# Fused pooled attention and rational MoE: zero-adding fill matmuls, shifted due times and a lead for the key transposes

## The chip, the cores and the metric

The kernel runs on one core of one Trainium2 chip. The metric is the time of one execution in device microseconds (us), the median of several runs. The profile is one further execution; its span is the time from the first instruction to the last.

## The reference, cut to what matters

Attention over keys and values pooled by 8, then a two-matrix network with a rational activation (all float32):

```python
B, H, S, D = 8, 8, 576, 64              # Sp = S // 8 = 72 pooled keys
k_p = k.reshape(B, H, Sp, 8, D).mean(axis=3);  v_p = v.reshape(B, H, Sp, 8, D).mean(axis=3)
attn = softmax(D ** -0.5 * q @ k_p.T)            # with 1e-9 added to the sum
x = (attn @ v_p).transpose(0, 2, 1, 3).reshape(4608, 512)
h = x @ w_in                                      # w_in 512 x 2048
g = (a0 + a1*h + a2*h**2 + a3*h**3) / (1 + |b0|*|h| + |b1|*h**2 + 1e-6)
out = g @ w_out                                   # w_out 2048 x 512
```

## The kernel before, in words

**Tiles.** The 4608 tokens are 18 blocks of 256. A block i goes through attention (scores `ps`, exponentials `e`, their transposes `pm` and `pr`, the split probabilities `am0` and `am1`, the products `pv`, and the split result `x0`, `x1`), then through 8 slices u of 256 hidden columns: `ph` = x times `win`u, the rational function on ScalarE, VectorE and GpSimd (tiles `t`, `w`, `r`, `rp`, giving `gh` and `gl`), and `po` += g times `wout`u. Float32 precision comes from splitting each operand in a high and a low part and adding three products. A `po` sum of a block takes two of the 8 PSUM banks (`po`i`_0`, `po`i`_1`) and stays open over its slices. The order table starts with blocks 0 and 1 on slices 0 to 3, then 2 and 3, while the weights still arrive; each weight is decoded (`m_win`, `m_wout`: ScalarE, then two VectorE instructions; then the high part by ScalarE and the low part by GpSimd).

**What sets the order.** The program isn't written in its final order. Each operation is recorded as an `Op` with a cost, its dependencies and a due time; `solve` moves due times backwards through the dependencies, then simulates the engines and always takes the operation that can start first, weighted a little by its due time. `issue` emits the operations in that order, so every engine runs a fixed list, in order, and waits on semaphores.

**The fill.** The planner also knows where TensorE has nothing to do. There `issue` puts matmuls of the identity (line 264 of the profile, tile `idle`) that nobody reads, one for each 0.12 us of the planned gap. They write the bank `idle`, which stays taken until a last operation on it that is due at 96; later, up to `FILL` = 110, they write the first bank of the next operation if that is still unused. All real work has line 267.

Of the kernel before, what the change touches and what calls it, by code (L numbers as in the profile page):

```python
# [8 lines left out]
F32 = mybir.dt.float32  # L9
F32R = mybir.dt.float32r  # L10
# [84 lines left out]
class Op:  # L95
    __slots__ = ("eng", "cost", "port", "calls", "deps", "users", "bufs", "due", "wait",
                 "ready", "seq", "bytes", "early", "slack", "start", "end")


class Plan:  # L100
# [5 lines left out]
    FILL = 110.0  # L106

    BETA = 0.02
# [13 lines left out]
    def add(self, eng, cost, calls, port=False, claims=(), bytes=0, early=34.0, after=()):  # L122
        op = Op()
        op.eng, op.cost, op.port, op.calls, op.bytes = eng, cost, port, calls, bytes
        op.early, op.slack = early, self.slack
# [28 lines left out]

    def solve(self):
        for op in reversed(self.ops):
            for d in op.deps:
                d.users.append(op)
                d.due = min(d.due, op.due - d.slack * (d.cost + 0.25 + (4.0 if d.bytes else 0.0)))
        for op in self.ops:  # L160
            op.wait, op.ready = len(op.deps), max(0.0, op.due - op.early)
# [9 lines left out]
        while done < len(self.ops):  # L171
# [35 lines left out]
            t, op = best  # L207
# [22 lines left out]
            for u in op.users:  # L230
                u.wait -= 1
                u.ready = max(u.ready, op.end + (self.LAT if u.eng != op.eng else 0.0))
                if not u.wait:
                    engs[u.eng].append(u)
# [4 lines left out]
    def issue(self):  # L239
        for op in self.order:  # L240
            for b in op.bufs:
                b.it = None
        engines = {"sp": self.nc.sync, "act": self.nc.scalar, "actq": self.nc.scalar,
                   "dve": self.nc.vector, "pool": self.nc.gpsimd, "pe": self.nc.tensor}
        value = lambda v: v.ap() if isinstance(v, Lazy) else v
        free, steady = None, [o.start for o in self.order if self.idle.tile in o.bufs][-1]
        for op in self.order:
            if op.eng == "pe" and op.start <= self.FILL:


                to = self.idle.ap() if op.start <= steady else None
                dst = op.calls[0][1][0]
                if to is None and dst.tile.it is None and dst.tile.dtype == F32:
                    to = dst.ap()
                one = self.filler
                if to is not None and tuple(to.shape) != (128, 128):
                    one = one.unsqueeze(1).to_broadcast([128, 2, 128])
                    if tuple(to.shape) not in ((128, 256), (128, 2, 128)):
                        to = None
                while free is not None and to is not None:  # L260
                    free += 0.12 if free > self.WARM else 0.215
                    if free > op.start - (0.0 if op.start <= steady else 0.2):
                        break
                    self.nc.tensor.matmul(to, lhsT=self.filler, rhs=one, start=True, stop=True)  # L264
                free = op.end
            for name, args, kw in op.calls:
                getattr(engines[op.eng], name)(*map(value, args),  # L267
                                               **{k: value(v) for k, v in kw.items()})
# [17 lines left out]
def tile_pooled_attention_then_rational_moe(  # L286
# [16 lines left out]
    nc = tc.nc  # L303
# [61 lines left out]
    ident = identr.bitcast(F32)  # L365
    masks = new("cpool", "masks", [P, 6], F32, "masks")
# [101 lines left out]
    def prep_k(n):  # L468
# [5 lines left out]
        for c0, c1, np in ((0, 2, P), (2, 4, P), (4, 5, H * SP - 4 * P)):  # L474
# [9 lines left out]
            while w > D:  # L484
# [8 lines left out]
            pe(109 * nc_, [  # L493
                ("transpose", (pk[:, (c0 + c) * P:(c0 + c + 1) * P] if c0 < 4 else pl[:, 0:np],
                               ks[:, c].rearrange("p a d -> p (a d)"), ident[:np, :np]), {})
                for c in range(nc_)])
        dst, both = kpT[n % 2], 2 * SP
# [407 lines left out]
    plan.now = 96.0  # L905
# [33 lines left out]
    plan.filler = identr  # L939
    plan.solve()  # L940
    with tc.manual_schedule():
        make_identity(nc, ones)
        nc.vector.tensor_copy(identr, ones)
        nc.gpsimd.memset(cbias, QC)
        plan.issue()
# [32 lines left out]
```

## Time and profile before

| | |
|---|---|
| median of 3 runs | 952.19 us (951.56 to 952.34) |
| the profiled execution's own time | 953.93 us |
| its span | 952.2 us |
| TensorE busy, fill matmuls included | 938.5 us |
| VectorE, ScalarE, GpSimd busy | 791.5, 691.6, 523.3 us |
| fill matmuls of 256 columns | 156 |

A fill matmul counts as busy. So the busy time of TensorE doesn't tell how much of it is work; its stretches with fill are read in the timeline, where a row is a run of like instructions with its start and length, and in brackets what the engine sat idle for before it.

### The profile page before, as it was taken

The page shows a single profiled execution, that of the slowest core. Times are in us where ns is not written, and L with a number is a line of the kernel's source. Part 1 is how long each engine was busy: PE and PEld are TensorE (multiplying, and loading weights), DVE is VectorE, ACT ScalarE, POOL GpSimd, SP SyncE. Part 2 cuts the span into 40 slices and gives each one's busy share as a digit, 9 for nine tenths or more (in the row PEclk, how much of TensorE's full clock was granted, in tenths as well). Part 3 has the DMA queues.
Part 4 walks back from the last instruction along what each step waited for, and adds up shares of the span by engine and source line. Part 5 has one row for each costly group of instructions (what it writes and reads, how often), then busy time and mean ns, then how long its engine had stood idle before and what let it go on. Part 6 is the DMA issues. An engine that isn't in the chain of part 4 may idle for free.

```text
span 952.2 us, 14488 instructions
## 1 busy us (share of the span) xinstructions
PE 938.5 (99%) x4888; PEld 786.1 (83%) x4888; DVE 791.5 (83%) x1334; ACT 691.6 (73%) x1124; POOL 523.3 (55%) x463
## 2 busy tenths in 40 slices
PE   8999999999999999999999999999999999999997
PEld 7989999898878888877887888878887888888886
DVE  6978888988898888888888989888979878886664
ACT  4778788687767686767777686858586868586764
POOL 4676667874456453547454844465456544444442
PEclk9999999999999999999999999999999999999999
DMA  9993110551436130316031512162223312020001
GB/s 280 345 384 120 24 50 1 120 149 49 89 64 148 19 60 12 66 51 141 5 68 50 122 33 43 41 135 55 32 53 74 71 26 53 0 56 1 23 1 45
DMA packets 185354, 75.16 MB, mean 79 GB/s; under 512 B 162624, under 2 KB 162624, under 8 KB 185280
## 3 DMA queue, kind: packets, MB, share of 16 engines
q1 hardware_dynamic: 185280, 74.23, 31.6%
q8 instruction: 39, 0.64, 0.3%
q14 instruction: 35, 0.29, 0.1%
HBM read 50.60 MB, written 12.58 MB: 66 GB/s over the span
## 4 chain that ended last, share of the span: by engine, by line
PE 84%; DVE 6%; ACT 3%; SPq 2%; DMA 2%; issue 2%; POOL 1%; ACTq 0%; POOLq 0%; DVEq 0%
PE po L267 37%; PE ph L267 36%; PE pv L267 4%; PE ps L267 3%; SPq L267 2%; DVE t L267 2%; PE idle L264 1%; DVE m_win L267 1%; DVE sm L267 1%; DMA q<-in_q_dram 1%; PE pvs L267 1%; DMA st_v<-in_v_dram 1%; DVE e L267 1%; ACT t L267 1%; ACT rp L267 1%
## 5 line engine op out<-in xcount | busy, mean ns | idle before, releaser
L267 PE MATMUL ph<-x,win 128*128 128x512 f32 (+1 forms) x2112 | 469.9, 354 | 4.8 <-DVE t L267 1.8
L267 PEld LDWEIGHTS ph<-x,win 128*128 128x128 f32 x2112 | 355.1, 188 | 72.6 <-DVE t L267 3.6
L267 PE MATMUL po<-wout,gh 128*128 128x512 f32 x1152 | 329.6, 397 | 0.3 <-ACT gh L267 0.3
L267 POOL TENSOR_TENSOR w<-w,r 128x512 f32<-128x512 f32 (+1 forms) x145 | 190.8, 1316 | 243.4 <-ACT r L267 228.9
L267 PEld LDWEIGHTS po<-wout,gh 128*128 128x128 f32 x1152 | 208.5, 188 | 42.1 <-ACT gh L267 0.5
L267 POOL TENSOR_TENSOR gl<-t,gh 128x512 fp32r<-128x512 f32 (+1 forms) x145 | 189.0, 1304 | 97.3 <-ACT gh L267 93.5
L267 PE MATMUL po<-wout,gl 128*128 128x512 f32 x576 | 167.6, 397 | 0.0
L267 ACT ACTIVATE t<-ph,abn 128x512 f32<-128x512 f32 (+1 forms) x145 | 111.7, 771 | 41.0 <-PE ph L267 30.8
L267 ACT ACTIVATE rp<-w,cbias 128x512 f32<-128x512 f32 (+1 forms) x145 | 99.7, 688 | 57.4 <-POOL w L267 24.3
L267 DVE TENSOR_TENSOR t<-t,ph 128x512 f32<-128x512 f32 (+1 forms) x145 | 98.4, 678 | 50.0 <-ACT t L267 48.0
L267 DVE SCALAR_TENSOR_TENSOR t<-t,abn,rp 128x512 f32<-128x512 f32 (+1 forms) x145 | 106.7, 736 | 35.2 <-ACT rp L267 33.8
L267 ACT ACTIVATE r<-w,abn 128x512 f32<-128x512 f32 (+1 forms) x145 | 117.7, 812 | 20.7 <-POOL gl L267 12.2
L267 PEld LDWEIGHTS po<-wout,gl 128*128 128x128 f32 x576 | 105.5, 189 | 21.9 <-issue 0.2
L267 DVE SCALAR_TENSOR_TENSOR t<-t,abn,ph 128x512 f32<-128x512 f32 (+1 forms) x145 | 107.5, 741 | 8.5 <-ACT w L267 4.7
L267 ACT ACTIVATE w<-ph 128x512 f32<-128x512 f32 (+1 forms) x145 | 85.9, 592 | 38.3 <-PE ph L267 29.8
L267 ACT CAST gh<-t 128x512 fp32r<-128x512 f32 (+1 forms) x145 | 88.4, 609 | 23.7 <-DVE t L267 23.4
L267 DVE SCALAR_TENSOR_TENSOR t<-rp,t 128x512 f32<-128x512 f32 (+1 forms) x145 | 99.0, 683 | 4.0
L267 DVE SCALAR_TENSOR_TENSOR rp<-w,rp 128x512 f32<-128x512 f32 (+1 forms) x145 | 99.2, 684 | 0.5 <-ACT rp L267 0.5
L267 ACT ACTIVATE rp<-rp 128x512 f32<-128x512 f32 (+1 forms) x145 | 84.1, 580 | 3.3 <-DVE t L267 0.5
L267 POOL TENSOR_TENSOR e<-e,sm 128x576 f32<-128x576 f32 x36 | 41.5, 1160 | 52.5 <-DVE sm L267 34.2
L267 PE MATMUL pv<-am,vm 128*128 128x256 f32 (+3 forms) x288 | 47.8, 278 | 0.5 <-ACT rp L267 0.4
L267 PEld LDWEIGHTS ps<-kpT,qT 128*128 128x128 f32 (+1 forms) x320 | 39.7, 178 | 9.5 <-issue 4.1
(95 smaller groups left out, 829.8 us busy)
## 6 DMA issues: line engine op xcount, KB each, us to landing
am<-e SPq DMA_DIRECT2D x224, 48.0 KB, 2.1
out_dram<-ob SPq DMA_DIRECT2D x17, 512.0 KB, 3.2
rwin<-in_moe_w_in_dram SPq DMA_DIRECT2D x8, 1024.0 KB, 11.8
rwout<-in_moe_w_out_dram SPq DMA_DIRECT2D x8, 1024.0 KB, 11.4
st_k<-in_k_dram SPq DMA_DIRECT2D x12, 512.0 KB, 4.8
st_v<-in_v_dram SPq DMA_DIRECT2D x12, 512.0 KB, 4.3
q<-in_q_dram SPq DMA_DIRECT2D x144, 32.0 KB, 2.1
st_v<-in_v_dram SPq DMA_DIRECT2D x48, 64.0 KB, 3.6
```

Of the source, the lines that this page charges most:

```text
L264: self.nc.tensor.matmul(to, lhsT=self.filler, rhs=one, start=True, stop=True)
L267: getattr(engines[op.eng], name)(*map(value, args), **{k: value(v) for k, v in kw.items()})
```

## The change

1. The operation that keeps the bank `idle` taken is due at `HEAD + 6` = 24 instead of 96. From there on the bank is one more for the work.
2. After that point a planned gap is filled, in the whole program and not only up to 110, with matmuls of the identity with a column of zeros (`zero`, broadcast to 256 columns) that add to a `po` sum that is open, with neither start nor stop. Where no sum is open, nothing is filled in.
3. `shift` goes over the first 2600 recorded operations eight times, each with its own seed, and moves the due time of some 3 in 100 by up to 4 either way.
4. The transposes of the pooled keys of batches 3 to 7 are planned with 1.5 us more after their operand.
5. Two short VectorE instructions at the start make the column of zeros.

```diff
+    MOVED, SHARE, REACH = 2600, 0.03, 4.0
+    SHIFTS = (827036, 619869, 758790, 768360, 308798, 563601, 635046, 970397)
...
+    def shift(self):
+
+        for seed in self.SHIFTS:
+            rnd = random.Random(seed)
+            for op in self.ops[:self.MOVED]:
+                if rnd.random() < self.SHARE:
+                    op.due += rnd.uniform(-self.REACH, self.REACH)
...
                 d.due = min(d.due, op.due - d.slack * (d.cost + 0.25 + (4.0 if d.bytes else 0.0)))
+        self.shift()
...
-                u.ready = max(u.ready, op.end + (self.LAT if u.eng != op.eng else 0.0))
+                u.ready = max(u.ready, op.end + u.lead + (self.LAT if u.eng != op.eng else 0.0))
...
-            if op.eng == "pe" and op.start <= self.FILL:
-                to = self.idle.ap() if op.start <= steady else None
-                dst = op.calls[0][1][0]
-                if to is None and dst.tile.it is None and dst.tile.dtype == F32:
-                    to = dst.ap()
...
+            if op.eng == "pe":
+                if op.start <= steady:
+                    to, one, first = self.idle.ap(), self.filler, True
                     one = one.unsqueeze(1).to_broadcast([128, 2, 128])
+                elif sums:
+                    to, one, first = list(sums.values())[-1][:, 0:256].ap(), self.zeros, False
+                else:
+                    to = None
                 while free is not None and to is not None:
                     free += 0.12 if free > self.WARM else 0.215
-                    if free > op.start - (0.0 if op.start <= steady else 0.2):
+                    if free > op.start:
                         break
-                    self.nc.tensor.matmul(to, lhsT=self.filler, rhs=one, start=True, stop=True)
+                    self.nc.tensor.matmul(to, lhsT=self.filler, rhs=one, start=first, stop=first)
                 free = op.end
+                for name, args, kw in op.calls:
+                    if name == "matmul" and args[0].tile.name.startswith("po"):
+                        sums[id(args[0].tile)] = args[0]
+                        if kw["stop"]:
+                            del sums[id(args[0].tile)]
...
+            turned.lead = 1.5 if n > 2 else 0.0
...
-    plan.now = 96.0
+    plan.now = HEAD + 6.0
     plan.add("pe", 0, [mm(plan.idle[:, 0], ident, ident, True, True)], early=0.0)
```

The diff shows the rules; what they do shows in the order. The changed program has 70 fill matmuls of 256 columns into `idle` (156 before) and 18 that add zeros: twice 3 around the products `pv2`, 4 in block 3's slices and 8 at block 4. All its other matmuls are those of before. From the last fill of 128 columns ahead of `pq2` on, TensorE has no fill until the first of these.

**TensorE, end of block 1's attention, before** (`pm`, `pr`: transposes of the exponentials `e1`; `pv1`: the products with the values; the fill writes `idle`):

```order
L267 MATMUL ph0_1_0_1_494<-x0_423,win1_426 128x256 x8
L267 MATMUL ph0_1_0_1_494<-x1_428,win1_426 128x256 x4
L267 MATMUL pm2_544<-identr_83,e1_447 128x128 x4
L264 MATMUL idle_98<-identr_83 128x256 x3
L267 MATMUL pm3_558<-identr_83,e1_447 128x128 x4
L264 MATMUL idle_98<-identr_83 128x256
L267 MATMUL pr2_568<-identr_83,e1_447 128x128 x2
L264 MATMUL idle_98<-identr_83 128x256 x2
L267 MATMUL pr3_576<-identr_83,e1_447 128x128 x2
L264 MATMUL idle_98<-identr_83 128x256 x23
L267 MATMUL pv1_0_621<-am0_1_572,vm00_308 128x256
```

The same place now (the line of real work is 283):

```order
L283 MATMUL ph0_1_0_1_475<-x0_424,win1_427 128x256 x8
L283 MATMUL pm2_539<-identr_83,e1_448 128x128 x4
L283 MATMUL ph0_1_0_1_475<-x1_429,win1_427 128x256 x4
L283 MATMUL pm3_552<-identr_83,e1_448 128x128 x4
L283 MATMUL pr2_560<-identr_83,e1_448 128x128 x2
L283 MATMUL pr3_573<-identr_83,e1_448 128x128 x2
L283 MATMUL pv1_0_588<-am0_1_557,vm00_311 128x256
```

The 29 fill matmuls are gone, and nothing stands in their place between `pr3` and `pv1`; four `ph` matmuls moved behind the first transposes.

**ScalarE at that place, before** (`e1` copied for the transposes, `am` made from them, `t0_1` the start of block 0's slice 1):

```order
L267 ACTIVATE t0_0_0_1_536<-ph0_0_0_1_450,abn_322 128x512
L267 ACTIVATE t0_1_0_1_549<-ph0_1_0_1_494,abn_322 128x512
L267 COPY e1_447<-e1_447 128x128 x4
L267 CAST am0_1_572<-pm2_544 128x4x128
L267 CAST am0_1_572<-pm3_558 128x4x128
L267 CAST am1_1_581<-pr2_568 128x2x128
L267 CAST am1_1_581<-pr3_576 128x2x128
```

And now:

```order
L283 ACTIVATE t0_0_0_1_536<-ph0_0_0_1_450,abn_327 128x512
L283 COPY e1_448<-e1_448 128x128 x2
L283 CAST am0_1_557<-pm2_539 128x4x128
L283 CAST am1_1_563<-pr2_560 128x2x128
L283 COPY e1_448<-e1_448 128x128 x2
L283 CAST am0_1_557<-pm3_552 128x4x128
L283 CAST am1_1_563<-pr3_573 128x2x128
```

`t0_1` moved behind `x0` of block 1, and the four copies are made in two pairs.

**TensorE at block 2's transposes, before** (`e2`: block 2's exponentials; `ph1_2`, `ph1_3`: block 1 on slices 2 and 3):

```order
L267 MATMUL ph1_3_0_1_1016<-x0_423,win3_815 128x256 x8
L267 MATMUL ph1_3_0_1_1016<-x1_428,win3_815 128x256 x4
L264 MATMUL idle_98<-identr_83 128x256 x12
L267 MATMUL pm4_1070<-identr_83,e2_928 128x128 x4
L264 MATMUL idle_98<-identr_83 128x256 x5
L267 MATMUL po0_0_0_744<-wout2_1056,gh0_2_0_1_1076 128x512
L267 MATMUL po0_0_1_746<-wout2_1056,gh0_2_0_1_1076 128x512
L264 MATMUL idle_98<-identr_83 128x256 x10
```

The same transposes now:

```order
L283 MATMUL ph0_3_0_1_875<-x0_424,win3_857 128x256 x4
L283 MATMUL pm4_948<-identr_83,e2_859 128x128 x4
L283 MATMUL ph0_3_0_1_875<-x0_424,win3_857 128x256 x4
L283 MATMUL ph0_3_0_1_875<-x1_429,win3_857 128x256 x4
L283 MATMUL ph1_2_0_1_806<-x1_429,win2_616 128x256 x4
L283 MATMUL ph1_2_0_1_806<-x0_424,win2_616 128x256 x8
L283 MATMUL ph1_3_0_1_992<-x0_424,win3_857 128x256 x4
```

The transposes moved ahead of the `ph` matmuls of slices 2 and 3, which now stand where the fill stood; behind them, six pairs of `po1` follow that before came later.

## Rows read from the trace of the kernel before

**Rows 1.** Part 1 of the page: busy time, share, instructions.

```profile
...
PE 938.5 (99%) x4888; PEld 786.1 (83%) x4888; DVE 791.5 (83%) x1334; ACT 691.6 (73%) x1124; POOL 523.3 (55%) x463
```

**Rows 2.** Groups of TensorE's instructions by form.

```profile
...
L264 PE MATMUL idle<-identr 128*128 128x256 f32 x156 | 25.1, 304 | 0.0
```

**Rows 3.** Windows by stage: length, five engines' busy time, PEclk, DMA share.

```profile
...
25.00:42.04 17.04, 15.73 (x133) 15.32 (x131) 16.05 (x27) 13.83 (x27) 13.68 (x11) 1.00 1.06 365
42.04:59.54 17.50, 17.00 (x128) 15.67 (x126) 16.34 (x21) 11.32 (x18) 11.06 (x9) 1.00 1.07 337
59.54:66.31 6.77, 6.77 (x30) 5.85 (x31) 3.58 (x7) 4.93 (x10) 6.49 (x3) 0.75 1.04 404
66.31:79.43 13.12, 13.12 (x108) 12.20 (x107) 11.51 (x24) 10.32 (x16) 6.37 (x5) 1.00 1.02 351
79.43:92.59 13.16, 13.16 (x107) 12.54 (x106) 10.78 (x18) 11.96 (x24) 10.29 (x7) 1.00 0.07 26
92.59:123.51 30.92, 30.92 (x207) 28.16 (x205) 25.98 (x44) 23.79 (x41) 20.89 (x19) 1.00 0.13 23
```

**Rows 4.** Timeline of TensorE, first part: start, length, instruction, wait.

```profile
...
30.37 0.97 PE L267 MATMUL ph<-x,win 128*128 128x256 f32 x6 [1.12 <-ACT x L267]
...
38.01 0.66 PE L267 MATMUL pm<-identr,e 128*128 128x128 f32 x4 [0.19 <-POOL e L267]
...
39.21 2.99 PE L264 MATMUL idle<-identr 128*128 128x256 f32 x23
42.04 0.40 PE L267 MATMUL pv<-am,vm 128*128 128x256 f32 x2
```

**Rows 5.** Timeline of ScalarE in the same part.

```profile
...
37.07 0.78 ACT L267 ACTIVATE t<-ph,abn 128x512 f32<-128x512 f32 x1 [0.24 <-PE ph L267]
37.74 0.89 ACT L267 COPY e<-e 128x128 f32<-128x128 f32 x4
```

**Rows 6.** Timeline of VectorE: two instructions of the head.

```profile
...
40.98 0.77 DVE L267 TENSOR_TENSOR am<-pr,am 64x256 fp32r<-64x256 f32 x2
...
53.93 3.16 DVE L267 TENSOR_SCALAR m_win<-m_win 128x1024 int32<-128x1024 int32 x1
```

**Rows 7.** Timeline of TensorE, second part.

```profile
...
55.93 2.05 PE L267 MATMUL pvr<-early,fourfold 32*128 32x128 f32 x16
57.91 1.13 PE L267 MATMUL pvs<-early,identr 128*128 128x256 f32 x4
59.54 1.16 PE L267 MATMUL ph<-x,win 128*128 128x256 f32 x4 [0.50 <-ACT win L267]
...
61.84 0.99 PE L264 MATMUL idle<-identr 128*128 128x256 f32 x2
62.62 0.83 PE L267 MATMUL po<-wout,gl 128*128 128x512 f32 x2
...
65.60 0.88 PE L264 MATMUL idle<-identr 128*128 128x256 f32 x6
```

**Rows 8.** Window of the slow clock, columns as in rows 3.

```profile
...
59.54:63.15 3.61, 3.61 (x12) 3.16 (x13) 2.18 (x5) 2.67 (x5) 3.59 (x2) 0.53 1.05 404
```

**Rows 9.** Timeline of TensorE, third part.

```profile
...
79.43 1.60 PE L264 MATMUL idle<-identr 128*128 128x256 f32 x12
80.87 0.60 PE L267 MATMUL pm<-identr,e 128*128 128x128 f32 x4
```

**Rows 10.** Timeline of GpSimd beside the long VectorE instruction.

```profile
...
54.02 1.29 POOL L267 TENSOR_TENSOR gl<-t,gh 128x512 fp32r<-128x512 f32 x1
55.27 1.27 POOL L267 TENSOR_TENSOR w<-w,r 128x512 f32<-128x512 f32 x1
```

**Rows 11.** What TensorE waited for after 130 us.

```profile
...
PE ph L267 <- DVE t L267: 1.8, 3, 0.9
...
PE ps L267 <- DVE kpT L267: 0.5, 1, 0.5
...
PE pk L267 <- DVE ks L267: 0.2, 1, 0.2
```

More of the change, by code (lines that the diff above doesn't have):

```diff
@@ L1 @@
+import random
 from contextlib import ExitStack
@@ L96 @@
     __slots__ = ("eng", "cost", "port", "calls", "deps", "users", "bufs", "due", "wait",
-                 "ready", "seq", "bytes", "early", "slack", "start", "end")
+                 "ready", "seq", "bytes", "early", "slack", "start", "end", "lead")
 class Plan:
@@ L104 @@
     WARM = 8.6
-    FILL = 110.0
     BETA = 0.02
+    MOVED, SHARE, REACH = 2600, 0.03, 4.0
+    SHIFTS = (827036, 619869, 758790, 768360, 308798, 563601, 635046, 970397)
     def __init__(self, nc):
@@ L124, in add @@
         op.eng, op.cost, op.port, op.calls, op.bytes = eng, cost, port, calls, bytes
-        op.early, op.slack = early, self.slack
+        op.early, op.slack, op.lead = early, self.slack, 0.0
         op.seq, op.due, op.deps, op.users = len(self.ops), self.now, set(), []
@@ L246, in issue @@
         free, steady = None, [o.start for o in self.order if self.idle.tile in o.bufs][-1]
+        sums = {}
         for op in self.order:
-            if op.eng == "pe" and op.start <= self.FILL:
-                to = self.idle.ap() if op.start <= steady else None
-                dst = op.calls[0][1][0]
-                if to is None and dst.tile.it is None and dst.tile.dtype == F32:
-                    to = dst.ap()
-                one = self.filler
-                if to is not None and tuple(to.shape) != (128, 128):
+            if op.eng == "pe":
+                if op.start <= steady:
+                    to, one, first = self.idle.ap(), self.filler, True
                     one = one.unsqueeze(1).to_broadcast([128, 2, 128])
-                    if tuple(to.shape) not in ((128, 256), (128, 2, 128)):
-                        to = None
+                elif sums:
+                    to, one, first = list(sums.values())[-1][:, 0:256].ap(), self.zeros, False
+                else:
+                    to = None
                 while free is not None and to is not None:
                     free += 0.12 if free > self.WARM else 0.215
-                    if free > op.start - (0.0 if op.start <= steady else 0.2):
+                    if free > op.start:
                         break
-                    self.nc.tensor.matmul(to, lhsT=self.filler, rhs=one, start=True, stop=True)
+                    self.nc.tensor.matmul(to, lhsT=self.filler, rhs=one, start=first, stop=first)
                 free = op.end
+                for name, args, kw in op.calls:
[3 more added lines that the diff above has]
+                            del sums[id(args[0].tile)]
             for name, args, kw in op.calls:
@@ L365, in tile_pooled_attention_then_rational_moe @@
     ident = identr.bitcast(F32)
+    zero = real([P, 1], F32R, tag="zero", name="zero")
     masks = new("cpool", "masks", [P, 6], F32, "masks")
@@ L492, in prep_k @@
                 in1=st[:, :, w:2 * w].unsqueeze(2).to_broadcast(both), op=ALU.add)
-            pe(109 * nc_, [
+            turned = pe(109 * nc_, [
                 ("transpose", (pk[:, (c0 + c) * P:(c0 + c + 1) * P] if c0 < 4 else pl[:, 0:np],
@@ L938, in tile_pooled_attention_then_rational_moe @@
         mm2(blocks, u, fs, gh, gl, halves)
-    plan.filler = identr
+    plan.filler, plan.zeros = identr, zero.to_broadcast([P, TOK])
     plan.solve()
@@ L943, in tile_pooled_attention_then_rational_moe @@
         nc.vector.tensor_copy(identr, ones)
+        nc.vector.memset(ones, 0.0)
+        nc.vector.tensor_copy(zero, ones[:, 0:1])
         nc.gpsimd.memset(cbias, QC)
```

## The prediction

> **What bounds the kernel now.** I first read the page's busy times: TensorE is busy 938.5 of 952.2 us, the others at most 83% [rows 1]. So its work sets the end, and the change, which removes no work, can only take away time in which TensorE does none: fill, waits, or a slow clock. The groups by form give the fill: 156 matmuls, 25.1 us of busy time [rows 2]. The order shows that the fill up to 25 us is nearly the same in both programs, so I then read TensorE's timeline from there on for fill and waits. Three places hold nearly all of it, and between 92.59 and 123.51 us TensorE is busy without a gap [rows 3], later it waits little [rows 11]. What is saved at these places is saved at the end, if TensorE stays fed behind them.
>
> Place A is the end of block 1's attention, where 23 fill matmuls stand between the last transposes and the products [rows 4]. Place B is where slice 3's weight comes late: a wait of 0.50 us, then a stretch of 3.61 us with a mean granted clock of 0.53, so nearly all of it at the lower level, 1.2 GHz, and 8 fill matmuls [rows 7, 8]. Place C is the wait for block 2's attention, with 45 fill matmuls between 79.43 and 92.59 us, the first 12 of which take the 1.44 us from 79.43 to 80.87, so 0.12 us each [rows 9].
>
> **The change, place by place.**
>
> *C.* All 45 are gone from the order, and `ph` and `po` work that came later stands there. 45 x 0.12 = 5.4 us less. This holds if that work's operands are there: the freed bank lets `ph` sums of block 1 start earlier, and block 2's transposes are asked for while they still have `ph` work behind them. Bounds: 0 (each fill turns into a wait) to 5.4. I take 5.4 here and count the new waits by themselves, below.
>
> *B.* The wait of 0.50, the two fills of 0.78 us (61.84 to 62.62, at the lower clock), the six of 6 x 0.12 = 0.72, and half of the remaining 3.61 - 0.78 = 2.83 us at half clock, 1.4 us: 3.4 us in sum [rows 7, 8]. Its cause: GpSimd ran two instructions from 54.02 to 56.54 us, and VectorE's first decode step of that weight, begun at 53.93, ended only at 57.09, after 3.16 us [rows 6, 10]. In the new order this step stands behind the decode of `wout1`, and TensorE has five more pairs of `po` matmuls and block 2's first scores ahead of `ph0_3`, which needs it. I take 3.4; bounds 0 and 3.4.
>
> *A.* The fill here hides a wait that stays: `pv1` needs the last low part, which VectorE ends at 40.98 + 0.77 = 41.75 us, and `pv1` starts at 42.04 [rows 4, 6]. Taking the fill away gives nothing by itself. What shortens the wait is that ScalarE's `t0_1` of 0.78 us no longer stands ahead of the copies, which start right behind it [rows 5]; the second transposes still wait for GpSimd (38.01 us) [rows 4]. I take 0.7; bounds 0 and 1.0 (0.78 and some of the 0.29 that the fill overshoots). The 1.12 us ahead of `ph0_0` [rows 4] stay, since nothing ahead of them moved but one fill.
>
> *What comes in.* The two times 3 zero fills around `pv2` cost 6 x 0.12 = 0.7 us (bounds 0, if they lie in a wait, and 0.7). A zero fill has the columns of the old one, so I use its time; no row shows one that adds. New waits: a list with no fill has nothing that absorbs an operand that is late. The waits of 25 to 93 us that show in spite of fill are 1.12 + 0.19 + 0.50 = 1.8 us [rows 4, 7]; I take 1.5 for the new ones in B and C, and as bounds 0 and 6.2 (what VectorE's rival below would make of it). The clock: TensorE now idles for most of 37 to 41 us. In the trace it fell after a part with narrow products and a wait of 0.50 us [rows 7], and stayed low for some 3.4 us (a mean of 0.53 over 3.61 us) [rows 8]; it did not show a fall around the wait of 1.12 us [rows 3, 4]. Such a fall costs half of 3.4 = 1.7 us of work; at an even chance 0.9 (bounds 0 and 3.4, two falls).
>
> The Trainium skill ("TensorE: Matmul & The Clock Gate", "HAM oscillation — how this bites in real kernels") says that TensorE left idle drops to half its clock and runs the next burst cold, and speaks against taking fill away. By it alone the fall would be certain, and the sum 0.8 us smaller; the trace agrees that a fall exists (0.53 for 3.61 us) and leaves open whether this gap causes one.
>
> *Behind the head.* The 12 zero fills at blocks 3 and 4 are new: 12 x 0.12 = 1.4 us, if the planned gaps aren't real. The lead for the key transposes aims at waits of 0.5 (scores on `kpT`) and 0.2 (`pk` on `ks`) [rows 11]: 0.7 less. Net 0.7 more. The eight lines of that view add up to 4.8 us, which the reshuffled order may save or double: bounds -4.8 and +6.2. DMA queues: the new order puts half of batch 1's keys behind `win3` and `wout1`, and `rwout3` behind the spill of block 0; the DMA engines are full until 79 us in both [rows 3], and none of these moved loads is needed by TensorE sooner than before, so I count 0. The two instructions for the column of zeros lie where VectorE waits for the first keys: 0.
>
> **The sum.** -5.4 (C) - 3.4 (B) - 0.7 (A) + 0.7 (zero fill) + 1.5 (new waits) + 0.9 (clock) + 0.7 (behind the head) = -5.7 us. The profiled execution took 953.93 us for a span of 952.2, which is 1.7 above the median; the saving is taken off the median: 952.19 - 5.7 = **946.5 us**.
>
> **The rivals.**
>
> *VectorE takes the bound.* From 42.04 to 92.59 us it is busy 16.34 + 3.58 + 11.51 + 10.78 = 42.2 of 50.55 us, 83% [rows 3]. My sum wants this stretch 3.4 + 5.4 - 0.7 - 1.5 - 0.9 = 5.7 us shorter, so 42.2 of 44.9 us, 94%. For it: VectorE's chain steps wait on each other's engines, and it has never been so full for so long. Against it: it was busy 16.05 of 17.04 us, 94%, from 25 to 42 [rows 3], and 2.5 us of its busy time was the late decode [rows 6]. Halfway, at 88%, the stretch takes 48.0 us: 2.6 us less, and about 949.6 us. Chance 0.15.
>
> A rule of the Trainium skill sharpens this ("SBUF — State Buffer", "Who interferes with whom"): a VectorE instruction that uses the port shared with GpSimd fully blocks while GpSimd holds it, and the one that issued first keeps it. The trace agrees: 3.16 us beside two GpSimd instructions. Which decode meets which GpSimd instruction now, no order tells.
>
> *The fill was only a picture of waits, and each comes back as one.* Then the change does nothing that counts: block 2's products wait for the same chain through ScalarE, VectorE and GpSimd. For it: in A just this happens. Against it: in C the order puts block 2's transposes in the middle of slice 3, not behind it. About 952 us. Chance 0.08.
>
> *The clock stays low: slower.* Without the 0.9 the saving is 6.6 us. Half clock costs half of the time that it lasts on work that TensorE has waiting, so beyond 13 us of it nothing is left, and beyond 17 us the kernel is slower by more than 0.2%. Were it low for 20 of the 37 us from 42 to 79: 952.2 - 6.6 + 10.0 = 955.6 us. For it: no fill stands between `pq2` and the first zero fill, and the clock did fall once even with fill. Against it: behind `pv1` the order is dense, and in dense parts the clock stayed at full level [rows 3]. Chance 0.07.
>
> **How the numbers follow.** My forecast has 0.70, with a range of its own of 943 to 949.5: the new waits and the clock between their bounds, place B at half or full. 0.2% of this kernel is 1.9 us, about what a measurement can tell from no change, so faster means below 950.3 and slower above 954.1. Faster: 0.70 and half of VectorE's rival, 0.77. Same: the other half and the fill that was only a picture, 0.16. Slower: the clock, 0.07. The range goes from the sum with no new cost in the head (5.4 + 3.4 + 1.0 and some of the 4.8 later, 941.5) to the rival in which nothing is gained, 952.0.
>
> **What would show it.** C is right if no wait over 1 us stands between `pv1` and `pv2`, and the work that was done at 92.59 us is done some 6 us earlier. B is right if TensorE doesn't wait for `win3` and the clock is 1.00 there. A: `pv1` starts near 41.3 us behind an idle time of about 1.7, and the windows behind it show whether the clock fell. VectorE's share from there to `pv2` tells the first rival. The prediction is wrong if waits of several us appear after 130 us, where I assumed that a reshuffled order waits as little as the old one.

## The result, and the profile after

The changed kernel takes 954.59 us (median of 9 runs, 953.63 to 956.81), the kernel before 952.34 us (951.56 to 953.29). The ratio is 1.0026 with a 95% interval of 1.0016 to 1.0037: slower by 2.5 us by the ratio, where 5.7 us less were forecast. The profiled execution took 956.46 us for a span of 954.8, so it lies in the upper part of its times.

Part 1 of the page and TensorE's groups by form, after; they answer to [rows 1] and [rows 2]:

```profile
PE 932.2 (98%) x4820; PEld 779.8 (82%) x4820; DVE 799.5 (84%) x1336; ACT 693.8 (73%) x1124; POOL 524.0 (55%) x463
```

```profile
L275 PE MATMUL idle<-identr 128*128 128x256 f32 x70 | 11.6, 318 | 0.0
L275 PE MATMUL po<-zero,identr 128*128 128x256 f32 x18 | 2.7, 275 | 0.0
```

TensorE is busy for 6.3 us less, so the fill did go. VectorE is busy for 8.0 us more with two short instructions more: its instructions got longer. Windows of the changed kernel, columns as in [rows 3]:

```profile
43.13:46.14 3.01, 3.01 (x15) 3.01 (x15) 2.98 (x3) 1.47 (x2) 2.34 (x1) 0.51 1.16 266
46.14:66.00 19.86, 19.86 (x145) 18.02 (x145) 17.82 (x26) 16.01 (x27) 11.46 (x10) 0.99 1.05 376
66.00:79.00 13.00, 12.19 (x89) 10.95 (x87) 12.24 (x26) 10.42 (x18) 10.62 (x7) 1.00 1.07 363
79.00:93.00 14.00, 14.00 (x95) 12.34 (x93) 11.84 (x17) 11.79 (x21) 9.40 (x7) 1.00 0.10 42
506.50:510.90 4.40, 1.74 (x8) 1.12 (x7) 4.40 (x8) 2.92 (x5) 1.32 (x1) 0.99 0.10 28
510.90:514.40 3.50, 3.50 (x10) 2.70 (x9) 3.43 (x6) 2.61 (x4) 2.52 (x2) 0.52 0.01 2
```

Two stretches of 3.0 and 3.5 us have half clock (columns 0.51 and 0.52), and ahead of the second TensorE works 1.74 of 4.40 us. Its timeline after, with the waits in brackets; the first five lines answer to [rows 4], 67.61 to the `ph0_3` of [rows 7], 84.39 and 86.34 are the zero fills around `pv2` at the place of [rows 9]:

```profile
30.68 0.98 PE L283 MATMUL ph<-x,win 128*128 128x256 f32 x6 [1.50 <-ACT x L283]
...
38.24 0.66 PE L283 MATMUL pm<-identr,e 128*128 128x128 f32 x4 [0.42 <-POOL e L283]
...
39.78 0.52 PE L283 MATMUL pr<-identr,e 128*128 128x128 f32 x2 [0.66 <-ACT e L283]
40.46 0.50 PE L283 MATMUL pv<-am,vm 128*128 128x256 f32 x2 [0.16 <-ACT am L283]
43.13 0.43 PE L283 MATMUL pv<-am,vr 128*64 128x256 f32 x1 [2.17 <-DVE am L283]
...
67.61 0.57 PE L283 MATMUL ph<-x,win 128*128 128x256 f32 x3
...
84.39 0.50 PE L275 MATMUL po<-zero,identr 128*128 128x256 f32 x3
...
86.34 0.52 PE L275 MATMUL po<-zero,identr 128*128 128x256 f32 x3
...
113.13 0.41 PE L283 MATMUL pr<-identr,e 128*128 128x128 f32 x2 [1.68 <-DVE t L283]
...
505.96 1.09 PE L283 MATMUL po<-wout,gh 128*128 128x512 f32 x4
509.72 1.20 PE L283 MATMUL ph<-x,win 128*128 128x512 f32 x4 [2.66 <-DVE t L283]
```

Place B has no wait for `win3`, place C none but 0.7 us of zero fill. The three long waits, at 43, 113 and 509 us, all end on VectorE. Its timeline at these places:

```profile
40.02 1.88 DVE L283 TENSOR_SCALAR m_win<-m_win 128x1024 int32<-128x1024 int32 x1
41.93 0.69 DVE L283 TENSOR_TENSOR am<-pm,am 128x512 fp32r<-128x512 f32 x1
42.65 0.43 DVE L283 TENSOR_TENSOR am<-pr,am 64x256 fp32r<-64x256 f32 x1
...
108.53 2.27 DVE L283 TENSOR_SCALAR sm<-sm 128x8 f32<-128x8 f32 x1
...
112.29 0.69 DVE L283 SCALAR_TENSOR_TENSOR t<-rp,t 128x512 f32<-128x512 f32 x1
...
500.06 0.71 DVE L283 STREAM_TRANSPOSE qT<-q 128x512 f32<-128x512 f32 x1 [2.34 <-DMA q<-in_q_dram]
500.70 1.34 DVE L283 TENSOR_TENSOR am<-am,am 128x1024 fp32r<-128x1024 f32 x1
...
504.04 1.69 DVE L283 TENSOR_TENSOR st_k<-st_k 128x512 f32<-128x512 f32 x1
...
506.85 1.82 DVE L283 TENSOR_TENSOR st_k<-st_k 128x256 f32<-128x256 f32 x2
...
508.93 0.74 DVE L283 SCALAR_TENSOR_TENSOR t<-t,abn,ph 128x512 f32<-128x512 f32 x1
```

And GpSimd's beside the first two:

```profile
39.38 3.09 POOL L283 TENSOR_TENSOR early<-early 64x256 f32<-64x256 f32 x3
...
108.37 2.40 POOL L283 TENSOR_TENSOR win<-m_win,win 128x1024 fp32r<-128x1024 f32 x1
```

In each place something long has come to stand ahead of the step that TensorE waits for. At 40 us it is the first decode step of `win2`, between the steps of `am1`; at 108 an addition on the 8 columns of `sm7`, ahead of three steps that free the bank for `pr6`; both run beside GpSimd. At 500 it is a transpose that waits for a DMA, and decode steps of batch 5's keys, ahead of the step (508.93) that frees a bank for `ph`.

How the two executions stand to each other: the moment at which the same number of columns of products that aren't fill has gone through TensorE, in the kernel named less in the kernel before (us, one profiled execution each; a 128x256 product has 256 columns; the variants are those below). From 112 us on the kernels compared have done the same products or nearly so; between 45 and 94 us the orders differ, and narrow products take more time per column than wide ones, so those rows are good to some 1 us only.

```
start before      after    nolead   noshift  move_507  nolead_moved  steady
          37      +0.46     +0.45     -0.08     +0.52         +0.59   +0.45
          45      +2.45     +2.50     -0.51     +2.20         -0.45   +0.77
          60      +1.82     +1.89     -0.69     +1.57         +1.00   +1.29
          79      +0.87     +0.92     -2.42     +0.63         +0.03   +0.31
          94      -5.13     -5.09     -4.37     -5.37         -5.98   -5.70
         112      -4.25     -4.17     -2.98     -4.47         -5.05   -4.80
         118      -2.25     -2.19     -2.99     -2.47         -4.92   -4.67
         285      -0.41     -1.03     -1.99     -1.02         -4.32   -4.38
         505      -1.72     -2.36     -1.53     -2.28         -5.72   -5.72
         516      +2.50     -1.64     +0.19     -2.57         -4.69   -5.50
         945      +2.54     -2.15     +1.36     -1.83         -4.81   -6.03
```

So the head has gained 4.25 us at 112, where the prediction had 6.4 (its sum without the term for what is behind the head). The 5.1 at 94 is partly the columns: TensorE waits for nothing between 94 and 112 us in either kernel. And some 1.7 of the 4.25 are the fall of the clock in place B of the kernel before [rows 8]. All of the gain is given back, and 2.5 us more: 2.0 us at 113, 1.8 between 118 and 285 (of which 1.3 come again by 505), and 4.2 at 509.

### The profile page after: what moved, and what is told of

Read it like the earlier page. It is cut to its first block, busy times and chain, and to the rows that moved or that the text cites. A ratio compares the mean times of both kernels' runs of the same rounds, so it can differ in the third digit from the quotient of the medians.

```text
span 954.8 us, 14344 instructions
## 1 busy us (share of the span) xinstructions
PE 932.2 (98%) x4820; PEld 779.8 (82%) x4820; DVE 799.5 (84%) x1336; ACT 693.8 (73%) x1124; POOL 524.0 (55%) x463
## 4 chain that ended last, share of the span: by engine, by line
PE 80%; DVE 9%; DMA 4%; SPq 2%; ACT 2%; issue 1%; POOL 0%; DVEq 0%; ACTq 0%; POOLq 0%
PE po L283 36%; PE ph L283 36%; PE pv L283 4%; PE ps L283 3%; DVE t L283 3%; DMA q<-in_q_dram 2%; SPq L283 2%; DVE sm L283 1%; DMA xd<-x 1%; DVE m_win L283 1%; DVE rp L283 1%; DVE am L283 1%; DVE st_k L283 1%; DMA ob<-pd 0%; DVE e L283 0%
## 5 line engine op out<-in xcount | busy, mean ns | idle before, releaser
L283 PEld LDWEIGHTS ph<-x,win 128*128 128x128 f32 x2112 | 350.4, 188 | 72.4 <-DVE t L283 6.6
L283 PEld LDWEIGHTS po<-wout,gh 128*128 128x128 f32 x1152 | 210.7, 189 | 44.9 <-DVE ob L283 1.3
L283 PE MATMUL po<-wout,gl 128*128 128x512 f32 x576 | 170.5, 397 | 0.0
L283 PE MATMUL ps<-kpT,qT 128*128 128x144 f32 (+1 forms) x320 | 46.0, 291 | 2.8 <-DVE kpT L283 1.4
```

What stands on the lines that cost most here:

```text
L283: getattr(engines[op.eng], name)(*map(value, args), **{k: value(v) for k, v in kw.items()})
```

## The experiments

The theory is that VectorE is late at these three places because of the new order, and that the clock falls behind two of the waits. The rivals: the zero fills cost the time; the lead and the seeds do harm everywhere; late DMAs would stall the kernel in any order. Times are medians, each ratio against runs of the kernel before on the same chip.

**The parts undone: nolead, noshift, noshift_nolead.**

```diff
-            turned.lead = 1.5 if n > 2 else 0.0
+            turned.lead = 0.0
```

```diff
-    SHIFTS = (827036, 619869, 758790, 768360, 308798, 563601, 635046, 970397)
+    SHIFTS = ()
```

> The changed kernel with the lead of the key transposes set to 0; bank release, seeds and zero fill stay. Its order up to 300 us is that of the changed kernel, and behind 495 us VectorE's order is again the old one (the decode st_k5_0 ahead of the transpose qT22, the product am1_10 behind t8_9_1_1). My theory: the lead put am1_10 and four st_k5 instructions between the transposes of qT22 and the step that frees a bank for ph8_9_3_1, and so made the 2.66 us wait at 509.72 and the half clock behind it, some 4.4 us together (lead curve -1.7 at 507, +2.8 at 514). Then this kernel takes about 950.2 us, with no PE wait over 1 us from 495 to 520. Rival (late keys and GpSimd there whatever the order): a wait of 2 us or more stays, 954 us. Rival (zero fill is the cost): 954 us too.

> The changed kernel without the moved due times; bank release, zero fill and lead stay. It has 37 zero fills in the head and 13 later. My theory: the seeds brought most of the head's gain (45 fills gone, 4.3 us at 94 us), and also both new collisions there (the decode of win2 among am1's steps at 40 us, the tiny sm7 step beside GpSimd's win4 at 108 us), so without them the program stands at about the old kernel's time at 130 us or up to 1.5 us ahead of it, and ends between 951 and 954 us depending on the lead's place at 507 us. Rival (the head's gain comes from the bank alone): ahead by 3 us or more at 94 us, and 949 us. Rival (each zero fill costs its 0.12 us and more): 50 x 0.12 = 6 us, so 957 us or more.

> The changed kernel without moved due times and without the lead: only the earlier release of the bank and the zero fill stay. My theory: the order from 300 us on is close to the old one, so no wait over 1 us at 495 to 520, and the time is the old kernel's less what the bank gives in the head: 950 to 952.5 us. Rival (zero fill costs 0.12 us each beyond waits, some 45 of them): 956 us. Rival (the bank alone gave the head's gain): 948 us.

Measured: nolead 952.40 us, 0.9998 (0.9989 to 1.0007); noshift 955.30, 1.0026 (1.0016 to 1.0036); both, 952.67, 0.9995 (0.9986 to 1.0003). The lead costs 0.0028 to 0.0031, 2.7 to 3 us, with seeds or without; its stall is gone in nolead (longest wait from 495 to 520 us: 0.4). In the profiles it costs more (4.2 from 505 to 516, against 0.7 in nolead). The seeds change nothing that can be measured. My theory had them bring most of the head's gain; by the table noshift, which has the bank, the zero fill and the lead, has 3.0 of the 4.25 us at 112, and what the seeds add is lost at 113. What the bank and the zero fill bring without the lead is open: noshift_nolead's profile has only 0.9 us there, with a fall of the clock at 42 us that noshift's doesn't have.

**Place 509: move_507, q_late.** Instructions are moved in the finished order; the numbers are those under which operations were recorded:

```diff
+    LATER = ((3325, 2858), (3249, 2878), (3253, 2878), (3248, 2878), (3252, 2878))
+    def move(self):
+        for what, past in self.LATER:
+            op = next(o for o in self.order if o.seq == what)
+            self.order.remove(op)
+            at = next(i for i, o in enumerate(self.order) if o.seq == past)
...
+            self.order.insert(at + 1, op)
...
     plan.solve()
+    plan.move()
```

> The changed kernel, lead and all, with five VectorE instructions at 500 us moved: the transpose of q11 behind t8_9_1_1's last step, and the four decode steps of st_k5 behind the step of t8_9_2_0 that frees the bank of ph8_9_3_1. My theory: that bank is free some 4 us earlier, there is no wait over 0.5 us at 509 and no half clock behind it, and the kernel takes what the one without lead takes or less: 952.2 us, down to 950.3 if the whole 4.4 us of the profile count. Rival (the lead does its harm elsewhere, for instance at 248, 282 or behind 520): 954.5 us.

> The changed kernel with one VectorE instruction moved: the transpose qT22 of the queries q11, which VectorE reaches before their DMA has landed (idle 2.34 us ahead of it at 500.06), now stands behind the last step of t8_9_1_1; the four decode steps of st_k5 stay where the lead put them. Theory a (the 2.3 us wait for the DMA is most of the stall at 509): the wait there falls to under 1 us and the half clock behind it goes, 952.2 us as with all five moved. Theory b (the decode steps, stretched beside GpSimd, are most of it): a wait of 1.5 us or more stays, 954 us. Theory c (both count, and the clock decides): in between, 953 us.

q_late has `((3325, 2858),)` alone. Measured: move_507 952.16 us, 0.9993 (0.9985 to 1.0002), with no wait at 509 and the clock at 1.00: with the lead still in, all that the lead cost is back. q_late 953.14, 1.0003 (0.9993 to 1.0013): the wait is 0.40 us.

```profile
506.87 1.19 PE L293 MATMUL ph<-x,win 128*128 128x512 f32 x4 [0.40 <-DVE t L293]
```

So the wait for `q11` is the larger part of the lead's cost (0.0023 of 0.0033). The median is that of theory c, but the 0.0010 that is left lies within the intervals, and the profile, of the quickest of its runs (951.93 us), looks like theory a. That the decode steps count too isn't shown.

**Places 43 and 113: move_a, move_113, win4_late.**

```diff
+    LATER = ((288, 252),)                  # move_a: first step of win2 behind am1
+    LATER = ((662, 544), (661, 544))       # move_113: sm7 behind the steps of t2_0_0_1
+    LATER = ((783, 663),)                  # win4_late: GpSimd's win4 behind the division by sm7
```

> The changed kernel with one VectorE instruction moved: the first decode step of win2 (128x1024), which stood between the steps of am1 and took 1.88 us there beside GpSimd's early1_0, now stands behind am1's last step. All other order is that of the changed kernel. My theory: pv1 waits for VectorE behind that step; am1's last steps then end at about 41.2 instead of 43.08, pv1 goes on at 41.3 instead of 43.13, and the half clock behind it (3 us, 1.5 us of cost) is gone or shorter: 1.8 to 3.3 us less, 951.3 to 952.8 us if nothing takes it back. Rival (late weights or GpSimd set the pace here, so the step's place is of no account): pv1 moves, but the gain is gone by 60 us, and the time is 954.5 us.

> The changed kernel with two tiny VectorE instructions moved (the addition to the sums sm7 and their reciprocal, 128x8), which at 108.53 us took 2.27 us beside GpSimd's win4 and held up the three steps that free a bank for pr6; they now stand behind these steps. My theory: the addition blocks on GpSimd and not on its own operands, so the steps end 2.3 us earlier, sm7 no later than now, and the wait of 1.68 us at 113.13 is gone: 1.7 us less, 953.0 us. Rival (sm7 sets what follows): the wait goes to another operand, 954.6 us.

> The changed kernel with one GpSimd instruction moved: the low part of win4 (128x1024), which ran from 108.37 to 110.77 us, now stands behind the division of e3 by sm7. VectorE's order is untouched, so the tiny addition on sm7 (128x8, 2.27 us) still stands ahead of the three steps that free a bank for pr6. My theory (the addition waits for GpSimd and does 0.4 us of its own at most): it takes 0.2 to 0.8 us now, pr6 no longer waits 1.68 us, and the time is that of the run where the addition was moved, 1 to 1.7 us less, 953 to 953.9 us. Rival (its length comes from its operands or its place in VectorE's list): it stays over 1.5 us, and the wait too, 954.9 us.

Measured: move_a 954.51 us, 1.0014 (1.0004 to 1.0023); move_113 954.87, 1.0013 (1.0003 to 1.0022); win4_late 955.36, 1.0025 (1.0016 to 1.0034). By the ratios the first two save some 1.1 us each, though their intervals overlap the changed kernel's. For move_a the clock on record speaks as well: a fall of 3.4 us at half clock takes 0.0018 off the mean clock of a run, and six of its 12 runs have a mean of 0.999 or 1.000, while none of the changed kernel's nine is above 0.998. The profile of move_a has a fall of the clock at 32 us, ahead of the place, that the changed kernel's doesn't have; so TensorE's timeline is shown of nolead_moved (below), which has the same move:

```profile
41.78 0.33 PE L293 MATMUL pv<-am,vr 128*64 128x256 f32 x1 [0.68 <-DVE am L293]
...
48.40 1.80 PE L293 MATMUL ph<-x,win 128*128 128x256 f32 x13 [1.27 <-DVE x L293]
```

The wait falls from 2.17 to 0.68 us and the clock stays at 1.00 from 43.13 to 46.14, but a new wait of 1.27 us follows (1.24 in move_a): the decode of `wout0`, 1.77 us beside GpSimd, stands ahead of the steps that make `x1`. So the rival holds in part. In move_113 TensorE waits for nothing at that place. VectorE in move_113 and, below it, in win4_late:

```profile
110.59 0.40 DVE L293 TENSOR_SCALAR sm<-sm 128x8 f32<-128x8 f32 x1
```

```profile
108.59 0.17 DVE L293 TENSOR_SCALAR sm<-sm 128x8 f32<-128x8 f32 x1
...
112.69 0.69 DVE L293 TENSOR_SCALAR ob<-po 128x512 f32<-128x512 f32 x1 [1.74 <-POOL win L293]
```

The same instruction on the same operands at the same place in VectorE's list takes 0.17 us instead of 2.27 when GpSimd's `win4` isn't beside it: the length was waiting for GpSimd, and the theory holds for the cause. It fails for the time. TensorE's wait there is not gone but 0.67 us, for another operand: the tile `ob` takes its buffer from the ring of `m_win` (one tag in the code), which `win4` frees when it ends; so `ob` waits 1.74 us, and `am1` behind it is as late as before. I had looked at the port alone, not at who waits for the moved instruction's buffer.

**The clock: gaps_filled, ph0_filled.** Zero fills in an open gap, inside a product's own sum (operations 253 and 134) or ahead of it, into an open `po` sum (2942):

```diff
+    ZEROS = {253: (2, 17), 2942: (0, 21)}   # gaps_filled; ph0_filled: {134: (2, 14)}
...
-            for name, args, kw in op.calls:
+            at, count = self.ZEROS.get(op.seq, (None, 0))
+            for n, (name, args, kw) in enumerate(op.calls):
+                if n == at:
...
+                    for _ in range(count):
+                        self.nc.tensor.matmul(to, lhsT=self.filler, rhs=self.zeros,
+                                              start=False, stop=False)
```

> The changed kernel with zero fills in its two longest gaps behind which the clock was at half: 17 between the second and third product of pv1 (gap of 2.17 us) and 21 ahead of ph8_9_3_1 (gap of 2.66 us). The work and its order on all other engines are unchanged. My theory (TensorE standing still is what the clock fell for, at 1.3 to 1.5 us for each fall): pv1 goes on at 43.1 and ph8_9_3_1 at 509.7 as before, but the clock is 1.00 from 43 to 46 and 510 to 515, and the time is 2.5 to 3 us less, 951.7 us. Rival (the fall has another cause, such as the narrow work ahead of the gap): half clock stays in both places, 954.7 us. Rival (fill matmuls delay the work): pv1 later by over 0.3 us, 955 us or more.

> The changed kernel with 14 zero fills inside ph0_0 (between its second and third product, where TensorE waits some 1.5 to 1.9 us for x0 from ScalarE at 28.9 to 30.7). In three of the profiles of other variants the clock fell to half behind this wait (32 to 35 us at 0.53), in the others not, at waits that are alike. Theory: without fill the fall is a lottery that costs 1.7 us in some executions, and is one reason why the changed kernel's times spread over 3 us (953.6 to 956.8) and the old one's over 1.7; with fill the slow half of them is gone: median 953.9, none over 955.5. Rival (the spread comes from elsewhere, such as the DMA of q11 at 500 us): the spread stays, median 954.7.

Measured: gaps_filled 953.42 us, 1.0007 (0.9999 to 1.0016). Timeline and windows (TensorE alone) of it:

```profile
41.03 2.06 PE L289 MATMUL pv<-zero,identr 128*128 128x256 f32 x17
43.34 0.33 PE L291 MATMUL pv<-am,vr 128*64 128x256 f32 x1 [0.24 <-DVE am L291]
```

```profile
43.13:46.14 3.01, 2.80 (x20) 1.00 1.17 272
510.90:514.40 3.50, 3.50 (x21) 1.00 0.00 0
```

`pv1` is no earlier, but the clock stays at its upper level, 2.4 GHz, in both places, and by the ratios 1.8 us are saved: TensorE standing still is what the clock fell for. Seven of its 11 runs have a mean clock of 1.000, none of the changed kernel's nine is above 0.998. The gain is smaller than the 2.5 to 3 us expected. ph0_filled 954.67 us, 1.0019 (1.0007 to 1.0030), spread 952.32 to 957.73: the spread didn't shrink, and that theory falls for the changed kernel. What does vary is place 509: in the profiles whose order there is that of the changed kernel and whose gap isn't filled (after, nozero, move_a, move_113, win4_late, ph0_filled), VectorE waits 1.8 to 3.9 us for `q11` and TensorE then 2.1 to 3.1 us, with half clock behind it in all but one. Over the runs of ph0_filled the time goes with the mean clock: 0.996 to 0.998 in the five up to 953.24 us, 0.993 to 0.996 in the seven from 954.65.

**The zero fills: nozero, bank_alone.**

```diff
-                elif sums:
-                    to, one, first = list(sums.values())[-1][:, 0:256].ap(), self.zeros, False
                 else:
                     to = None
```

> The changed kernel without the 18 zero fills; everything else, the order of the real work too, is the same. My theory: most of them lie where TensorE would wait anyway or cost their 0.12 us, so 0 to 2 us less: 953.5 us, and the waits at 43, 113 and 509 us stay. Rival (they are the cost): 951 us or less. Rival (they keep the clock up): a stretch of half clock appears behind block 3 or 4, and the time is 956 us or more.

> The changed kernel with neither moved due times, nor lead, nor zero fill: the earlier release of the bank is all that is left. Against the run with its 50 zero fills (0.9995) it prices them: if each costs its 0.12 us, 6 us less, 946.6 us; my theory, from the 18 fills that were worth about 0.9 us, is that half lie in gaps that exist anyway: 2 to 3 us less, 950 us. Rival (they keep the clock at full level): half clock appears behind the gaps that they filled, and the time is 952.5 us or more.

nozero is the changed kernel, bank_alone noshift_nolead, each without zero fill. Measured: nozero 954.20 us, 1.0016 (1.0005 to 1.0026), 0.9 us less than with fill, within the intervals; bank_alone 955.62, 1.0030 (1.0011 to 1.0049), 3.3 us more than with it (0.9995). TensorE in bank_alone, timeline and window:

```profile
86.33 0.44 PE L281 MATMUL pr<-identr,e 128*128 128x128 f32 x2 [1.28 <-DVE am L281]
87.69 1.11 PE L281 MATMUL pq<-identr,q 128*128 128x128 f32 x4 [0.92 <-DVE am L281]
```

```profile
87.00:91.00 4.00, 3.16 (x10) 0.57 0.00 0
```

This profile is of the quickest of bank_alone's eight runs, so it doesn't show where the median loses 3.3 us; the mean clocks do. They go from 0.998 at 951.89 us down to 0.989 at 959.83, while noshift_nolead's 11 runs lie between 0.996 and 0.998. At 0.998 the times are alike: 951.89 and 952.02 without the fills, 951.69 to 953.09 with them. The fills (48 in the trace of noshift_nolead) cost next to nothing and held the clock: the rival is right, my 2 to 3 us less were wrong.

Of the 18 fills of the changed kernel four stand at 181 us, ahead of a wait. TensorE there in the changed kernel and, below it, in nozero, with nozero's window:

```profile
180.81 0.61 PE L275 MATMUL po<-zero,identr 128*128 128x256 f32 x4
182.33 1.21 PE L283 MATMUL ph<-x,win 128*128 128x256 f32 x8 [0.91 <-DVE t L283]
```

```profile
184.28 1.21 PE L281 MATMUL ph<-x,win 128*128 128x256 f32 x8 [1.93 <-DVE t L281]
```

```profile
185.47:188.88 3.41, 3.41 (x14) 0.50 0.00 0
```

So without them the clock fell at block 3, which the rival had named. It is one execution, the slowest of nozero's 12 (959.33 us); the median is that of my theory. So these fills can save a fall, and in the other executions they cost at most their 2 us.

**Do the causes add up: nolead_moved, x_first, x_first_nozero, best, steady.** nolead_moved is nolead with the moves of move_a and move_113. The others add to it:

```diff
+    LATER = (..., (162, 258))      # x_first: the step of wout0 behind the steps of x1
+    LATER = (..., (3325, 2903))    # best: qT22 later; no zero fill
+    ZEROS = {134: (2, 14), 263: (2, 10)}   # steady: zero fills ahead of ph0_0's and x1's waits
```

> The changed kernel without the lead, with the step of win2 behind am1's last step and the two sm7 instructions behind t2_0_0_1's, as in the two runs before. My theory: the three places add up: 952.4 (measured without the lead) less 1.8 to 3.3 and 1.7, so 947.4 to 948.9 us, faster than the old kernel by over 3 us. Rival (what is saved before 115 us is lost to late VectorE behind it): 951.5 us or more.

> The run without lead with win2's step and the sm7 instructions moved (950.6 us, 0.9972), and one more VectorE instruction moved: the first decode step of wout0 (1.77 us at 43.99 beside GpSimd) now stands behind the two steps that make x1. There ph waited 1.27 us for x1 at 48.40. My theory: x1 is done 1.7 us earlier and that wait is gone: 1.2 us less, 949.3 us. Rival (wout0 is then late for the first po, or the step blocks on GpSimd's win2 in its new place): the wait comes back at 58 us as <-ACT wout, and the time stays at 950.5 us.

> The kernel of the run before (x1 first) without the zero fills. My theory: fills cost a little (about 0.7 us less without the 18 of the changed kernel) and none of them keeps the clock up in this order, so 0.5 to 1 us less than with them. Rival (here they hold the clock in the gaps of blocks 2 and 4): a stretch at half clock appears, and it takes 1 us or more longer.

> The run without lead with win2's step and the sm7 instructions moved (0.9972), without zero fills, and with qT22 moved behind the steps of t8_9_2_0 and t8_9_2_1. My theory: the fills give 0.5 to 1 us, and a late q11 can no longer hold up VectorE at 500 us: 0.9960 to 0.9965, 948.7 to 949.2 us. Rival (no fill costs the clock somewhere): a stretch at half clock appears in the profile, and it is 950.6 us or more.

> The run without lead with win2's step and the sm7 instructions moved (0.9972), and zero fills in its two longest gaps of the head: 14 ahead of the third product of ph0_0, 10 in the 1.27 us wait for x1 at 48 us. Theory: the waits stay, the clock no longer falls behind them in any execution: median 949.5 to 950 us, and no time above 951.5. Rival (the fall there is rare or the fills delay the work): 950.6 us or more.

Measured: nolead_moved 950.57 us, 0.9972 (0.9961 to 0.9983): faster than before, the two moves save 2.5 us together, less than the 3.5 to 5 expected. x_first 951.65, 0.9987 (0.9975 to 0.9999), and without zero fill 950.12, 0.9967 (0.9954 to 0.9979). x_first is slower than its theory had it (949.3 us), and its timeline and window show the rival that I had named:

```profile
59.60 1.22 PE L293 MATMUL po<-wout,gh 128*128 128x512 f32 x2 [1.68 <-ACT wout L293]
```

```profile
59.60:63.00 3.40, 3.40 (x9) 0.53 1.03 409
```

The wait for `x1` is gone and comes back as one for `wout0`, with a fall of the clock. Its zero fills can't be priced from the pair: the wait ahead of `qT22` was 4.03 us in x_first's profile and 2.15 in the other's. best 953.04, 0.9992 (0.9981 to 1.0003): `qT22`, moved as late as that, stands ahead of the last step of `am1_10`; the steps behind it are late in turn, and TensorE waits 2.1 us at 511. The rival's half clock is there as well, behind the wait ahead of `ph0_0` (shown further down) and at 512. steady 947.89 (947.49 to 948.82), 0.9951 (0.9939 to 0.9963): the fastest, 4.7 us under the kernel before and 7 under the changed one. Behind 25 us it has no unfilled wait over 0.7 us. The fills stand in the two waits (28.94 and 48.07), but half clock shows from 41.3 to 44.7 us all the same. So its 2 us beyond nolead_moved aren't those of my theory: the mean clock is 0.998 to 0.999 in its five runs and 1.000 in four of nolead_moved's seven (949.11 to 950.57 us), and in the table, one execution of each, it draws ahead of nolead_moved only behind 505 us, far from the fills. Where they come from is open.

```profile
28.94 1.73 PE L299 MATMUL ph<-zero,identr 128*128 128x256 f32 x14
...
48.07 1.28 PE L299 MATMUL ph<-zero,identr 128*128 128x256 f32 x10
```

## Why the prediction was wrong

*C (-5.4)* was right: from 79 us to 112, where both have done the same products again, the difference goes from +0.87 to -4.25, 5.1 us less, with the zero fills around `pv2` (+0.7) already in it.

*B (-3.4)* was right in its cause and too large: no wait for `win3`, clock 0.99; from 45 to 79 us it brought 2.45 - 0.87 = 1.6 us net of the new waits there (0.28 ahead of `pq5` and 0.5 for `vr`). And the slow clock of that place, more than half of the term, belongs to the profiled execution, not to the median. Of the 134 runs of the kernel before that were timed beside the variants, 124 have a mean clock of 0.999 or 1.000, so no such fall; the other ten took 953.65 to 955.92 us. The profiled one took 953.93, at 0.997. The 1.7 us by which it lay above the median fit this one fall, and the prediction took what the fall costs off a median that doesn't have it.

*A (-0.7)* was wrong. I watched ScalarE's `t0_1` and not VectorE's list, where a decode step had come between the steps of `am1`: `pv1` goes on at 43.13, not 41.3. With the clock (3.01 us at 0.51, 1.5 us) A costs 2.45 - 0.46 = 2.0 us, where 0.7 less were forecast. The wait ahead of `ph0_0`, which was to stay at 1.12, is 1.50.

*The clock (+0.9)* was half of one fall; in the profile there are two, 1.5 us here and 1.7 at 509 (3.50 us at 0.52). With mean clocks of 0.996 to 0.998 each of the changed kernel's nine runs has at least one, and gaps_filled, without the two, gets 1.8 of the 2.5 us back.

*Behind the head (+0.7)* is the step that failed: there I assumed that a reshuffled order waits as little as the old one, with the lead saving 0.7. From 112 us to the end the profile, 1.9 us above its kernel's median, loses 4.25 + 2.54 = 6.8 us, past the bound of 6.2. The lead, meant to save 0.7 us, costs 2.7 by the ratios (nolead), through five VectorE instructions that it moved ahead of the step that frees a bank; the collision at 113 costs about 1.1 (move_113; 2.0 in the profile). The wait at 182 us (0.91) stands in the kernel before too; what those at 248 and 282 are due to wasn't tried.

*The rivals.* VectorE's was nearest: from 43.13 to 93 us it is busy 2.98 + 17.82 + 12.24 + 11.84 = 44.9 of 49.9 us, 90%, and at 43 and 113 us it is held up beside GpSimd. It was given 949.6 since I looked for it in the head only. The Trainium skill ("SBUF — State Buffer", "Who interferes with whom") says that where a VectorE instruction uses the ports shared with GpSimd, the one that issued first keeps them and the other fully blocks; the trace agrees: 2.27 us against 0.17. The fill as a picture of waits holds for A and for the zero fills of bank_alone, not for C. The clock staying low for 20 us did not happen. A head gain that is lost again and turns into a slower kernel was in none of them.

## What to carry to other kernels

When a table of numbers or a lead reorders a list, look at what comes to stand ahead of each step that frees a bank or ends a wait, on the engine that does that step; a lead on TensorE's key transposes made its stall through five instructions of VectorE. Fill that lay in a real wait cost next to nothing here and kept falls of the clock away (gaps_filled, bank_alone), so take away the wait before the fill. Before a fall of the clock in one profile is counted as a saving, look at the mean clock of the other runs: if they don't have the fall, the median has nothing to give back. Ask of each moved instruction who waits for its result and for its buffer: four of the moves here traded one wait for another.

## What the runs showed of the hardware that was not expected

- A VectorE addition on 128x8 took 0.17 us alone and 2.27 beside a GpSimd instruction of 2.40 us. The planner knows the shared port for the decodes, not for this one.
- The clock falls behind some waits and not behind others of the same length. Behind 1.86 us ahead of `ph0_0` it held in nolead; behind 1.87 in best it fell; behind 1.68 it held at 113 us (after) and fell at 59.6 (x_first). nolead, then best, each timeline and window:

```profile
30.68 0.97 PE L283 MATMUL ph<-x,win 128*128 128x256 f32 x6 [1.86 <-ACT x L283]
```

```profile
31.00:34.00 3.00, 3.00 (x27) 1.00 1.04 405
```

```profile
30.57 1.48 PE L291 MATMUL ph<-x,win 128*128 128x256 f32 x6 [1.87 <-ACT x L291]
```

```profile
31.00:34.00 3.00, 3.00 (x15) 0.50 1.05 410
```

Most falls lasted some 3.4 us, at 1.2 GHz, so some 1.7 us of work. Two lasted twice that: one in nozero from 42.1 us, and this one in x_first_nozero:

```profile
57.80:64.60 6.80, 6.17 (x19) 0.50 1.04 405
```
